# Scripting the start of a DeltaNet and feed-forward kernel: counted conversion steps, denser score evacuations, weight fetches from another queue

## The chip, the core and the metric

The kernel runs on one core of a Trainium2 chip. The time is device microseconds (us) of that core for one execution. Below, VectorE, ScalarE, TensorE and GpSimd are the core's compute engines, and SP is the engine that here only issues transfers (DMAs). Each engine works off its own queue of instructions in order: an instruction that waits holds all that stand behind it in the same queue (in run e8 below one ScalarE step waits 10.78 us for its tile, and the copies behind it come late).

Single executions of one kernel spread over some 1 to 7 us, so medians are quoted with the profile's own span beside them where a trace is argued from.

## The reference, cut to what matters

```python
k_n = k / (norm(k) + 1e-6)                       # q, k, v: (4, 8, 768, 48), float32
for t in range(768):                             # the delta rule, per batch and head
    y[t]  = q[t] @ state
    v_old = state @ k_n[t]
    state = state + beta[t] * outer(k_n[t], v[t] - v_old)
x  = y as (3072, 384)
xn = x / sqrt(mean(x * x) + 1e-6) * rms_g
out = (silu(xn @ w_gate) * (xn @ w_val)) @ w_out # weights are float64: 384x1536, 384x1536, 1536x384
```

The kernel works in chunks of 128 tokens. A unit is one chunk of one batch, so there are 24 units, four to a chunk. For each chunk, K is normalized and transposed, scores are formed on TensorE, the diagonal blocks of the scores are gathered through DRAM into one tile (`gblk`), all 32-by-32 blocks are inverted together on VectorE (31 steps of two operations), and the result is scattered back through DRAM (`td`, `tt`, `nd`, `ne`). Then a short recurrence of matmuls gives each unit's outputs, and the feed-forward follows. The weights arrive as 64-bit words and are turned to float32 by hand: 18 tiles, five VectorE operations and one ScalarE operation each, some 4 us of VectorE a tile.

## The kernel before

The four parts that the change touches. Everything of the first chunk is a generator in one plan with a time for each step; the program's order on each engine comes from these planned times.

```python
def fetch():                                     # one raw weight tile, 768 KB, three buffers
    ...
    nc.sync.dma_start(out=to, in_=src)           # SP's queue, with all other loads

def keys(to, p_g):                               # K's scores, 8 copies a unit, all on ScalarE
    nc.scalar.copy(to[:, :, K0], p_g[:, :, K0])
    nc.scalar.copy(to[hi, :, K1], p_g[hi, :, K1])

def gather(n):                                   # four transfers a unit, issued by ScalarE
    for a in range(NBLK):
        nc.scalar.dma_start(out=gds[c][...], in_=gp[b][W * a : W * (a + 1), :, o : o + W])
    if b == B - 1:
        nc.sync.dma_start(out=gblk, in_=gds.pop(c))
# ... cut ...
TF = 68                                          # planned start of the feed-forward
at(0, setup())
for n in range(B):
    at(0, prepare_first(n, ...))
at(20.9, invert(0, 0.74))
at(49, recur(0, 1.5, 3))                         # units 0,1 and then 2,3
for i, m in enumerate((0, 1, 0, 1)):
    at(TF + CYC // 4 * i, ffn(m, ...))
at(0, weights([(12 + 4.2 * i, 0.8) for i in range(2)] + [(46 + 4.2 * i, 0.8) for i in range(5)]
              + [(TF + 1 + 3.1 * i, 0.6) for i in range(11)]))
```

The preparation of a later unit, which plays a part in the end, is the same in both kernels:

```python
def normalize(n):
    nc.scalar.square(ksq, kn)                    # ScalarE
    nc.vector.tensor_reduce(out=ksum, in_=ksq)   # VectorE
    nc.gpsimd.tensor_scalar_max(ksum, ksum, 1e-30)
    nc.gpsimd.tensor_tensor(out=knrm, in0=ksum, in1=half, op=ALU.pow)   # GpSimd, 1.7 to 2.7 us
    yield
    nc.vector.tensor_scalar_add(knrm, knrm, 1e-6)                       # VectorE waits for it
    nc.vector.reciprocal(krec, knrm)
    ...
def prepare(n):
    norm_k = normalize(n)
    next(norm_k); yield 1.5; next(norm_k); yield 2.5
    transpose(n, qpad[n % 2], Q0);  yield 3
    transpose(n, kpad[n % NK], K0); yield 2
    score(n, ..., both)                          # its masks are VectorE operations
    yield 1
    gather(n)
```

Of the kernel before, what the change touches and what calls it, by code (L numbers as in the profile page):

```python
# [21 lines left out]
W = 32  # L22
# [5 lines left out]
def kernel(  # L28
# [105 lines left out]
    def setup():  # L134
        for t in kpad + qpad:
            nc.vector.memset(t[:, :, D:DP], 0.0)
        for n in range(B):
            load_k(n)
        fetch()

        beta_sb = ttb.rearrange("p k j -> p (k j)")[0:BH, 0:S]
        nc.sync.dma_start(out=beta_sb, in_=beta.rearrange("b h s -> (b h) s"))
        blocks = beta.rearrange("b h (c a i) -> a (b h) c i", a=NBLK, i=W)
        for a in range(NBLK):
            nc.sync.dma_start(out=nbeta[a * BH : (a + 1) * BH], in_=blocks[a])
        load_q(0)
        fetch()
        load_q(1)
        fetch()
        nc.sync.dma_start(out=g_sb, in_=moe_rms_g.rearrange("(t p) -> p t", p=128))  # L150
        nc.vector.memset(half, 0.5)
        nc.vector.memset(mhalf, -0.5)
        make_identity(nc, ident)
        row, col = (
            gblk.bitcast(I32).rearrange("p k j -> p (k j)")[:, C * i : C * (i + 1)] for i in (0, 1)
        )
        nc.gpsimd.iota(row, pattern=[[0, 128]], base=0, channel_multiplier=1)
        nc.gpsimd.iota(col, pattern=[[1, 128]], base=0, channel_multiplier=0)
        nc.vector.memset(mask[lo, 1], 1.0)
        for i, p in enumerate((lo, hi)):  # L160
            nc.vector.tensor_tensor(
                out=mask[p, i], in0=row[p, p], in1=col[p, p], op=ALU.is_lt
            )
        p_fill.append(psum.tile([128, DM], FP32, name="p_fill", tag="out", bufs=2))
        stay_warm(14)
        yield 15
        nc.vector.tensor_scalar(
            out=nbeta, in0=nbeta, scalar1=-1.0, scalar2=None, op0=ALU.mult
        )
        yield 3  # L170
        p_bt = ps_delta([128, NCH, BH], "p_bt")
        for c in range(NCH):
            nc.tensor.transpose(
                p_bt[:, c], beta_sb[:, c * C : (c + 1) * C], ident[0:BH, 0:BH]
            )
        nc.scalar.copy(beta_t, p_bt)
        yield 5
        for n in range(B):
            load_v(n)
        load_k(B)  # L180
        yield 3
        nc.scalar.memzero(tt_all)
        yield 4
        nc.scalar.memzero(gp_all[HC:C, :, 0:HC])
        yield 4
        for t in state:
            nc.scalar.memzero(t)


    p_fill = []  # L190
# [26 lines left out]
    def fetch():  # L217
        i = len(raws)
        if i < len(todo):
            raw = bits.tile([128, WT], I64, name="raw", bufs=3)  # L220
            src = todo[i][1]
            to = raw if len(src.shape) == 2 else raw.rearrange("p (n m) -> p n m", m=DM)
            nc.sync.dma_start(out=to, in_=src)
            raws.append(raw)

    def words(raw):
# [9 lines left out]
        nc.scalar.activation(out=top, in_=high.bitcast(FP32), func=ACTF.Copy, scale=2.0**-112)  # L236
        return top

    def weights(times):
        clock, tops = 0, []  # L240
        for i, ((dst, src), raw, (time, dt)) in enumerate(zip(todo, raws, times)):
            yield time - clock
            clock = time + 5 * dt
            if i == 0:
                tops.append(shrink(raw))
            low, high = words(raw)
            top = tops[i]
            top_u, dst_u = top.bitcast(U32), dst.bitcast(U32)
# [5 lines left out]
                op0=ALU.logical_shift_left,  # L254
                op1=ALU.bitwise_and,
            )
            yield dt
            nc.vector.scalar_tensor_tensor(
                out=top_u,
                in0=high,  # L260
# [2 lines left out]
                op0=ALU.bitwise_and,  # L263
                op1=ALU.bitwise_or,
            )
            yield dt
            if i + 1 < len(todo):
                tops.append(shrink(raws[i + 1]))

            nc.vector.tensor_scalar(  # L270
                out=dst_u, in0=top_u, scalar1=0xFF800000, scalar2=None, op0=ALU.bitwise_and
            )
            yield dt
            nc.vector.scalar_tensor_tensor(
                out=dst, in0=low, scalar=2.0**-52, in1=dst, op0=ALU.mult, op1=ALU.mult
            )
            fetch()
            yield dt
            nc.vector.tensor_tensor(out=dst, in0=dst, in1=top, op=ALU.add)
            yield dt  # L280
        bits_pool.close()


    def normalize(n):
# [66 lines left out]
        keys(to, p_g)  # L351
        queries(to, p_g)

    def bare_queries(to, p_g):
        nc.scalar.copy(to[lo, :, Q0], p_g[lo, :, Q0])
        nc.scalar.copy(to[:, :, Q1], p_g[:, :, Q1])

    def gather(n):
        c, b = divmod(n, B)
        if b == 0:  # L360
            gds[c] = dram.tile([128, W, W], FP32, name="gd")
        for a in range(NBLK):
            o = diagonal(a)
            nc.scalar.dma_start(
                out=gds[c][a * BH + b * H : a * BH + (b + 1) * H].rearrange("h r j -> r h j"),
                in_=gp[b][W * a : W * (a + 1), :, o : o + W],
            )
        if b == B - 1:
            nc.sync.dma_start(out=gblk, in_=gds.pop(c))
# [20 lines left out]
        gather(n)  # L390


    def prepare_first(n, times):
        norm_k = normalize(n)
        yield times[0]
        next(norm_k)
        yield times[1]
        next(norm_k)
        yield times[2]
        transpose(n, kpad[n % NK], K0)  # L400
        yield times[3]
        score(n, crossed((0, slice(K0, K0 + 1)), (1, slice(K0, None, 2))), keys)
        gather(n)
        yield times[4]
        transpose(n, qpad[n % 2], Q0)
        load_q(n + 2)
        yield times[5]
        score(n, crossed((0, slice(Q0, None, 2)), (1, slice(Q1, Q1 + 1))), bare_queries)
        yield times[6]
        for place, p in ((Q0, lo), (Q1, hi)):  # L410
            part = gp[n][p, :, HC * place : HC * (place + 1)]
            nc.vector.tensor_tensor(
                out=part, in0=part, in1=mask[p, place // 2, None].to_broadcast([HC, H, HC]), op=ALU.mult
            )
# [4 lines left out]
    def invert(c, dt):  # L419
# [19 lines left out]
                stay_warm(2, tmp_b[:, 0 : min(128, n * (i + 1))])  # L439
            yield dt  # L440
        if c == 0:
            stay_warm(22)
        td = dram.tile([128, W, W], FP32, name="td")
        nd = dram.tile([128, W, W], FP32, name="nd")
        nc.sync.dma_start(out=td, in_=ttb)
# [32 lines left out]
            if n + B < NU:  # L478
                load_v(n + B)

    def recur(c, dt, warm=0):
        units = range(B)
        vss, x2s, p_zs, us = {}, {}, {}, {}

# [139 lines left out]
        ys = {}  # L624
        if c == 0:

            for a, b in ((0, 1), (2, 3)):
                corner(a, None)
                stay_warm(warm)
                yield dt  # L630
                corner(b, a)
                yield dt
                inner(None, None, a)
                corner(None, b)
                yield dt
                inner(a, None, b)
                stay_warm(warm)
                yield dt
                inner(b, a, None)
                stay_warm(warm)  # L640
                yield dt
                u_a = us[a]
                outer(None, a)
                yield dt
                inner(None, b, None)
                stay_warm(warm)
                yield dt
                u_b = us[b]
                outer(None, b)
                yield dt  # L650
                transpose_y(a, scale(*ys.pop(a)))
                stay_warm(warm)
                yield dt
                transpose_y(b, scale(*ys.pop(b)))
                stay_warm(warm)
                yield dt
                update(a, u_a)
                yield dt
                update(b, u_b)
                reload()  # L660
                dt, warm = 1.2, 0
                yield dt
            return
        for s in range(-3, B + 2):
            inner(s, s - 1, s + 1)
# [98 lines left out]
        yield 0.1  # L764



    plan = []

    def at(time, gen):  # L770
# [2 lines left out]
    def run_plan(until=math.inf):  # L773
        heap = plan
        heapq.heapify(heap)
        while heap and heap[0][0] < until:
            t, i, gen = heapq.heappop(heap)
            dt = next(gen, None)
            if dt is not None:
                heapq.heappush(heap, (t + dt, i, gen))  # L780


    TF = 68
    CYC = 3 * FT * B // 2
    at(0, setup())
    for n in range(B):

        times = (3.5 + 1.2 * n, 6.6 + 1.7 * n, 7.4 + 1.8 * n, 9.3 + 1.8 * n, 24 + 4 * n, 26 + 4 * n, 46.5 + 3 * n)
        at(0, prepare_first(n, [b - a for a, b in zip((0,) + times, times)]))
    at(20.9, invert(0, 0.74))  # L790
    at(49, recur(0, 1.5, 3))
    half_f = FT // 2
    for i, m in enumerate((0, 1, 0, 1)):
        at(TF + CYC // 4 * i, ffn(m, half_f * (i // 2), half_f * (i // 2 + 1)))
    at(
        0,
        weights(
            [(12 + 4.2 * i, 0.8) for i in range(2)]
            + [(46 + 4.2 * i, 0.8) for i in range(5)]
            + [(TF + 1 + 3.1 * i, 0.6) for i in range(11)]  # L800
        ),
    )
    for c in range(1, NCH):
        t0 = TF - 16 + CYC * c
        first = TF + 2 if c == 1 else t0 - 60
        for b in range(B):
            at(first + 4.5 * b, prepare(B * c + b))
        at(first + 27, invert(c, 0.68))
        at(*((t0 - 4, recur(c, 0.9)) if c == 1 else (t0 - 9, recur(c, 1.2))))
        for g in range(B // 2):  # L810
            at(t0 + 16 + CYC // 2 * g, ffn(B // 2 * c + g, 0, FT))
    with tc.manual_schedule():
        run_plan(TF + CYC // 2)
    run_plan()


# [28 lines left out]
```

## Time and profile before

The median is 883.5 us in three runs. The page and the stretches are shown in the prediction, from the same trace (span 881.3 us).

| mark in the trace of before | us |
|---|---|
| first inversion step (VectorE) | 35.33 |
| inversion ended (start of the product after it) | 62.47 |
| first p_w of unit 0 on TensorE | 73.02 |
| first feed-forward matmul | 103.58 |
| TensorE idle from there to 260 | 10.1 |
| clock lost from there to 215 | 4.5 |

Idle is the length of a stretch less TensorE's busy time. Clock lost is the length times one less the mean granted clock; the clock is given to two digits, so it is good to about 0.6 us. Idle time at a low clock counts in both.

### The profile page before, as it was taken

How to read it: one execution, taken by the hardware profiler on the slowest of the kernel's cores; microseconds unless marked ns; L12 is line 12 of the kernel's file. 1: busy time of each engine (PE TensorE's matmuls, PEld its weight loads, DVE VectorE, ACT ScalarE, POOL GpSimd, SP SyncE). 2: the span in 40 equal slices, each digit the busy share in tenths (PEclk: the TensorE clock that was granted, in tenths of full speed). 3: DMA queues.
4: the chain of work that ended last, by engine and by line, in shares of the span. 5: the costliest groups of instructions: out<-in, count | busy, mean ns of one | idle time of the engine just before them, and what ended most of it. 6: DMA issues, size and time to landing. Idle time of an engine off the chain costs nothing.

```text
span 881.3 us, 19880 instructions
## 1 busy us (share of the span) xinstructions
PE 828.5 (94%) x8434; PEld 646.7 (73%) x8434; DVE 404.7 (46%) x997; ACT 259.0 (29%) x691; POOL 97.7 (11%) x136
## 2 busy tenths in 40 slices
PE   6487798989999999999999999999999999999998
PEld 5376665767877777787777787777787777777776
DVE  3786677886243393243392243492332491221110
ACT  4622345511424312324311324212334212221101
POOL 3000144200041000131000131000130000010000
PEclk8576799999999999999999999999999999999999
DMA  7615536502222103122103122103121103000000
GB/s 182 169 45 133 145 98 157 151 2 75 57 56 49 46 18 86 31 63 39 47 18 85 38 56 41 46 18 85 39 55 23 36 23 80 2 20 1 18 1 18
DMA packets 150935, 51.81 MB, mean 59 GB/s; under 512 B 142368, under 2 KB 145440, under 8 KB 150848
## 3 DMA queue, kind: packets, MB, share of 16 engines
q1 hardware_dynamic: 124736, 47.40, 21.2%
q10 hardware_dynamic: 26112, 3.15, 2.2%
q8 instruction: 66, 1.08, 0.5%
q14 instruction: 21, 0.17, 0.1%
HBM read 36.37 MB, written 14.16 MB: 57 GB/s over the span
## 4 chain that ended last, share of the span: by engine, by line
PE 72%; DVE 9%; DMA 2%; ACT 2%; issue 1%; POOL 1%; ACTq 0%; SPq 0%
PE p_gv L732 36%; PE p_o L719 18%; DVE tmp L428 4%; DVE ttb L437 3%; PE p_g L329 3%; PE p_y L531 2%; PE p_t L313 2%; PE p_k L569 2%; PE p_z L587 2%; PE p_y L569 2%; PE p_x L605 1%; PE p_v L497 1%; PE p_z L596 1%; DMA gblk<-gd 1%; PE p_s L550 1%; DVE h_f L743 1%
## 5 line engine op out<-in xcount | busy, mean ns | idle before, releaser
L719 PE MATMUL p_o<-wo_sb,h_f 128*128 128x384 f32 x576 | 215.8, 497 | 11.1 <-DVE h_f L743 11.1
L732 PE MATMUL p_gv<-xt,wg_sb 128*128 128x256 f32 x864 | 217.3, 388 | 0.0
L732 PE MATMUL p_gv<-xt,wv_sb 128*128 128x256 f32 x864 | 213.6, 383 | 0.0
L732 PEld LDWEIGHTS p_gv<-xt,wg_sb 128*128 128x128 f32 x864 | 161.6, 193 | 39.4 <-issue 0.6
L732 PEld LDWEIGHTS p_gv<-xt,wv_sb 128*128 128x128 f32 x864 | 161.5, 190 | 24.4 <-issue 2.5
L743 DVE TENSOR_TENSOR h_f<-sil,p_gv 128x256 f32<-128x256 f32 x144 | 60.1, 418 | 241.3 <-ACT sil L741 241.1
L741 ACT ACTIVATE sil<-p_gv 128x256 f32<-128x256 f32 x144 | 55.1, 383 | 342.8 <-PE p_gv L732 314.7
L719 PEld LDWEIGHTS p_o<-wo_sb,h_f 128*128 128x128 f32 x576 | 104.0, 190 | 62.7 <-DVE h_f L743 16.7
L428 DVE SCALAR_TENSOR_TENSOR tmp<-gblk,nbeta,ttb 128x31 f32<-128x31 f32 (+15 forms) x186 | 74.7, 402 | 11.5 <-DMA gblk<-gd 4.7
L437 DVE TENSOR_TENSOR ttb<-ttb,tmp 128x31 f32<-128x31 f32 (+15 forms) x186 | 63.6, 342 | 6.6 <-PE p_g L329 0.5
L343 DVE TENSOR_TENSOR gp<-p_g,mask 64x128 f32<-64x128 f32 (+1 forms) x160 | 37.9, 277 | 40.0 <-ACT gp L339 35.6
L329 PE MATMUL p_g<-kqt 64*64 64x192 f32 (+2 forms) x896 | 46.3, 331 | 9.5 <-ACT gp L339 4.8
L329 PEld LDWEIGHTS p_g<-kqt 64*64 64x64 f32 x896 | 34.1, 147 | 20.1 <-ACT gp L339 6.5
L293 POOL TENSOR_TENSOR knrm<-ksum,half 128x8 f32<-128x8 f32 x24 | 42.4, 1765 | 2.0
L688 POOL TENSOR_SCALAR ms<-ms 128x1 f32<-128x1 f32 x24 | 5.9, 247 | 328.0 <-ACT y L680 327.8
L318 ACT COPY kqt<-p_t 128x512 f32<-128x512 f32 x48 | 28.0, 584 | 40.2 <-PE p_t L313 37.9
L420 POOL MEMSET ttb<- 128x1024 f32 x6 | 6.1, 1021 | 261.5 <-DMA td<-ttb 246.0
L587 PEld LDWEIGHTS p_z<-v_raw,tt 64*64 64x64 f32 x768 | 26.1, 142 | 8.8 <-issue 6.7
L512 ACT COPY vs<-p_v 32x256 f32<-32x256 f32 x48 | 17.4, 362 | 49.4 <-PE p_w L504 28.1
L338 ACT COPY gp<-p_g 128x128 f32<-128x128 f32 x96 | 25.5, 265 | 20.3 <-PE p_g L329 18.4
L605 PE MATMUL p_x<-tt,gp 64*64 64x64 f32 x384 | 29.0, 229 | 1.8 <-ACT tt L514 1.8
L531 PE MATMUL p_y<-u,gp 128*64 128x48 f32 x768 | 26.6, 222 | 3.4 <-DVE u L612 3.2
(87 smaller groups left out, 798.6 us busy)
## 6 DMA issues: line engine op xcount, KB each, us to landing
kpad<-in_k_dram SPq DMA_DIRECT2D x24, 192.0 KB, 2.6
raw<-in_moe_w_gate_dram SPq DMA_DIRECT2D x6, 768.0 KB, 5.0
qpad<-in_q_dram SPq DMA_DIRECT2D x24, 192.0 KB, 2.8
raw<-in_moe_w_val_dram SPq DMA_DIRECT2D x6, 768.0 KB, 4.7
v_raw<-in_v_dram SPq DMA_DIRECT2D x24, 192.0 KB, 3.0
raw<-in_moe_w_out_dram SPq DMA_DIRECT2D x6, 768.0 KB, 4.3
out_dram<-o_sb SPq DMA_DIRECT2D x24, 192.0 KB, 1.9
gd<-gp ACTq DMA_DIRECT2D x96, 32.0 KB, 1.7
```

Source lines behind the costliest of these rows:

```text
L293: nc.gpsimd.tensor_tensor(out=knrm, in0=ksum, in1=half, op=ALU.pow)
L329: nc.tensor.matmul(to, pair[d, K1 if i else K0], pair[d, places], skip_group_check=True)
L343: nc.vector.tensor_tensor(out=to[p, :, place], in0=p_g[p, :, place], in1=mask[p, i, None].to_broadcast([p.stop, 2, HC]), op=ALU.mult,)
L428: nc.vector.scalar_tensor_tensor(out=tmp, in0=gblk[:, i, None, i + 1 :].to_broadcast(shape), scalar=nbeta[:, c, i : i + 1], in1=ttb[:, 0 : ...
L437: nc.vector.tensor_tensor(out=to, in0=to, in1=tmp, op=ALU.add)
L531: nc.tensor.matmul(p_y[p, h], gp[b_y][:, h, HC * place : HC * (place + 1)], u[:, h], start=(c == 0 and h == 0), stop=True, skip_group_chec ...
L587: nc.tensor.matmul(p_zs[b_z][p, h], tt[b_z][p, h], r[p, h], start=(h == 0), stop=(p is lo), skip_group_check=True,)
L605: nc.tensor.matmul(p_x[lo, h], gp[b_x][hi, h, HC * K0 : HC * (K0 + 1)], tt[b_x][hi, h], skip_group_check=True,)
L719: nc.tensor.matmul(p_o[i], h_f[:, i * C : (i + 1) * C], wo_sb[:, f], start=(f == f0), stop=(f == f1 - 1),)
L732: nc.tensor.matmul(p_gv[:, i], w_sb[:, t, f * 128 : (f + 1) * 128], xt[:, t], start=(t == 0), stop=(t == KT - 1),)
L741: nc.scalar.activation(out=sil, in_=p_gv[:, 0], func=ACTF.Silu)
L743: nc.vector.tensor_tensor(out=h_f, in0=sil, in1=p_gv[:, 1], op=ALU.mult)
```

## The change

Its intent: start the feed-forward sooner. (1) The first chunk becomes a script, and instead of planned times the script says after which instruction how many conversion steps stand on VectorE. (2) K's scores of a unit go to two PSUM banks and leave in four larger copies, two on VectorE and two on ScalarE; SP issues the gathers. (3) All but the first three weight fetches are issued by GpSimd. (4) The second chunk's planned times move. The diff, cut to its core:

```diff
-            nc.sync.dma_start(out=to, in_=src)
+            (nc.sync if i < 3 else nc.gpsimd).dma_start(out=to, in_=src)
...
+        dma = (nc.scalar if c > 0 else nc.sync).dma_start      # in gather
...
+    def keep_keys(n, p_gs):
+        for par in range(2):
+            nc.vector.tensor_copy(out=heads(n, par, K0), in_=p_gs[par][:, :, 0])
+            nc.scalar.copy(heads(n, par, K1)[hi], p_gs[par][hi, :, 1])
+        gather(n)
... the recurrence of units 0 and 1, in one go; 2 and 3 stay in the plan
+            corner(0, None); stay_warm(3); convert(1)
+            corner(None, 0); stay_warm(2); corner(1, None)
+            inner(None, None, 0); convert(1)
... 
+            transpose_y(1, scale(*ys.pop(1)))
+            convert(4)
+            yield
+            update(0, u_0)
...
+        for n in range(B):                                     # in begin
+            p_gs = score_part(n, K0)
...
+            keep_keys(n, p_gs)
+            convert((1, 2, 2, 5)[n])
...  the second chunk; its old places, counted from the feed-forward's start,
...  were 2 + 4.5 * b, 29 with 0.68, 52 with 0.9, and 36 planned units in manual order
+            at((8 if c == 1 else t0 - 76) + 4.5 * b, prepare(B * c + b))
+        at(35 if c == 1 else t0 - 49, invert(c, 0.62))
+        at(*((57, recur(c, 0.7)) if c == 1 else (t0 - 25, recur(c, 1.2))))
+        run_plan(60)
```

## The prediction

> **What bounds the kernel now.** I read the granted clock and busy slices over the span first, then a table by stage, then the engines' timelines up to 104 us.
>
> From the page of the kernel before, each digit one of 40 slices of 22 us:
>
> ```profile
> PE   6487798989999999999999999999999999999998
> ...
> PEclk8576799999999999999999999999999999999999
> ```
>
> TensorE is full from about slice 10 on and neither full nor at full clock before. The table by stage (stretch, its length, then busy us and instruction count of PE, PEld, DVE, ACT and POOL, the granted clock, DMA share, GB/s):
>
> ```profile
> 0.00:36.00 36.00, 21.83 (x218) 17.20 (x218) 16.46 (x42) 20.94 (x56) 10.14 (x18) 0.74 0.65 171
> 36.00:63.00 27.00, 17.05 (x162) 14.22 (x163) 23.09 (x61) 9.84 (x33) 0.00 (x0) 0.65 0.36 75
> 63.00:104.00 41.00, 29.61 (x535) 27.24 (x534) 30.84 (x42) 11.87 (x28) 2.69 (x4) 0.73 0.46 135
> 104.00:200.00 96.00, 86.36 (x671) 65.17 (x671) 74.02 (x158) 38.24 (x92) 23.11 (x21) 0.95 0.40 105
> 200.00:860.00 660.00, 655.73 (x6783) 509.61 (x6782) 258.18 (x692) 175.44 (x478) 61.75 (x93) 1.00 0.18 42
> ```
>
> From 200 us on TensorE idles 4 us in 660: that part can't get shorter, for the change takes no matmul out of it. All to be won lies before the first feed-forward matmul at 103.58 us, and in the 9.6 us of idle (96.00 - 86.36) and the lost clock between 104 and 200. The end is therefore: start of the feed-forward, plus the matmuls left by then, plus TensorE's later idle.
>
> The marks of the path to 103.58, from the timelines of the engines (start, duration in us, engine, what; the wait before it in brackets):
>
> ```profile
> 14.49 1.86 ACTq L364 DMA_DIRECT2D gd<-gp  x4
> ...
> 28.84 1.82 ACTq L364 DMA_DIRECT2D gd<-gp  x4
> ...
> 31.94 0.34 SPq L369 DMA_DIRECT2D gblk<-gd  x1
> ...
> 35.33 0.25 DVE L428 SCALAR_TENSOR_TENSOR tmp<-gblk,nbeta,ttb 128x31 f32<-128x31 f32 x1 [3.61 <-DMA gblk<-gd]
> ...
> 62.47 1.96 DVE L447 TENSOR_TENSOR gblk<-ttb,nbeta 128x1024 f32<-128x1024 f32 x1
> ...
> 84.83 0.56 DVE L612 TENSOR_TENSOR u<-p_z,beta_t 64x384 f32<-64x384 f32 x1 [2.64 <-PE p_z L596]
> ...
> 90.75 0.56 DVE L612 TENSOR_TENSOR u<-p_z,beta_t 64x384 f32<-64x384 f32 x1
> ...
> 103.58 2.68 PE L732 MATMUL p_gv<-xt,wg_sb 128*128 128x256 f32 x6
> ```
>
> K is normalized, transposed and scored (to 28.84), gathered through DRAM (gblk issued at 31.94), inverted on VectorE (35.33 to 62.4, 27.1 us), scattered, and then units 0 and 1 run the recurrence. In the K part ScalarE is the serial engine: from 12.52 to 30.66 it does four times eight small evacuations (0.26 to 0.27 us each, 2.3 us a unit) and four times the issue of four gathers (1.8 us a unit, during which its queue does nothing else). That is 16.4 of the 18.1 us.
>
> **What the Trainium skill says.** "TensorE: Matmul & The Clock Gate", Part 1 (the HAM clock gate): the clock is halved after an idle window of about 3.4 us and restored after a busy one. The trace agrees: the granted clock is 0.65 and 0.73 in the second and third stretch, and four 128x128 transposes take 0.66 us at full and 1.11 at half clock. So the fills stay useful, and idle costs more than its length.
> "DMA: Bandwidth & Descriptors", section "Issuing engines are not separate DMA queues": SP, ScalarE and GpSimd feed the same 16 DMA engines, and another issuer saves sequencer time alone. Hence the gathers moved to SP should land no sooner after issue (median 1.7 us here), but ScalarE gets 1.8 us a unit back; and weight loads issued earlier by GpSimd will share the DMA engines with the gathers.
> "SBUF — State Buffer", section "SBUF: two separate sides": a DMA issued by GpSimd needs descriptors that it can't write while VectorE runs a two-port operation. No fetch is issued by GpSimd in the trace before, so it shows nothing of this. The 128x768 tensor_scalar steps (0.56 us) are candidates for such a lock, and they surround every fetch.
>
> **The change part by part.**
>
> 1. K's scores. A unit's evacuation becomes two VectorE copies of 128x256 and two ScalarE copies of 64x256. From rows reading PSUM (128x256 on VectorE 0.42, 32x256 on ScalarE 0.36) I take 0.40 and 0.37: 0.8 us and 0.75 us side by side, in place of 2.3 us on one engine; the four issues go to SP. ScalarE stops being the bound. But in ScalarE's new order the fourth square stands behind the first transposed copy (end 9.5), so the fourth reduce ends at about 10.6, and in VectorE's order it stands before unit 1's normalization: 11.55 instead of 10.24. From there by hand: transpose of unit 1 to 12.7 (half clock), score 0 to 14.7, its copies to 15.6, one conversion step 0.56, normalization of unit 3 0.93, score 1 to 17.8, copies to 18.6, two steps (0.96 + 0.56) to 20.2, score 2 to 20.9, copies to 21.7, two steps (0.96 + 0.96) to 23.7, copies of unit 3 to 24.5, SP's four issues 1.85 to 26.3, last landing 1.3 later as before (30.66 to 31.94) at 27.6, gblk 3.4 as before: 31.0. Nearby weight loads may add 0.8. The inversion starts at 31.8 and not 35.3: 3.5 us saved. The inversion itself is the same 62 operations: no change.
>
> 2. The recurrence of units 0 and 1. The scatter chain behind the inversion is the same (td, tt, nd, ne by SP), so unit 0's p_w can start hardly before its 10.4 us. From there the script helps: p_w of unit 0 no longer shares its loop with p_v of unit 1, so p_x starts about 1.3 us sooner; and VectorE's order is chosen by hand. Before, u of unit 1 waited from 88.1 (its p_z done) to 90.75 behind a mask and three conversion steps: 2.6 us. In the new order only the mask stands between, and both gains together bring that u from 90.75 to about 86. Following p_y, square, pow, scale, transpose with the old durations (1.2, 0.7, 1.6, 0.6, 0.8) and a fill of 0.9 puts the last x-transposed at about 92 on the old clock of the inversion's end. Then the feed-forward starts at once; before it waited for both state updates and the corners of units 2 and 3, to 103.58. This moves 11.4 us, but the moved matmuls (64 for the states, about 2.4 us, and 96 for the corners, about 2.2) are still to be done, and the sixth weight tile is converted only at about 95.4, a stall of up to 1.2. Left: 11.4 - 4.6 - 1.0 = 5.8 us.
>
> 3. Weight fetches by GpSimd. Before, ScalarE waited 4.5 us for a raw tile at 86.4, because SP's queue was full of scatters; that wait ends. It was beside the path, so it counts only within part 2. Against it, two fetches now fall into the scatter: I take off 0.5 us.
>
> 4. The middle, 104 to 200. Conversions before the feed-forward: six tiles instead of seven and a half, but the rest is done (12 x 3 = 36 units of the plan) about when the second inversion starts (35), while before the two overlapped and h_f stood behind both (3.8 us of idle between 174 and 190, with a half-clock window after it). The second recurrence starts later and runs denser (0.7 for 0.9 a step), which can give a little back. I credit 2 us of the 9.6 plus lost clock.
>
> Sum: 3.5 + 5.8 - 0.5 + 2 = 10.8 us, so 883.5 - 10.8 = 872.7; I say 872.
>
> **The rivals.**
> a) The second recurrence becomes the bound: with fewer feed-forward blocks to hide its chain, TensorE idles around 190 to 230 and the gain of the start is given back. For: in the old trace this stretch has no slack to lose (0.4 us of idle in 200 to 250), and the chain runs through ScalarE and VectorE. Against: the plan ends it at the same time. It would give 878 to 884.
> b) Fetches by GpSimd are late or block GpSimd's queue, where the pow of the norms and the clearing of ttb stand behind them (ttb is cleared after the second fetch, by my count at about 30, one us before it is needed). A slip of 2 us each at the inversion and in the scatter makes 876 to 878.
> c) All of the middle's stalls go: 9.6 us of idle and some 5 of half clock in three windows of 3.4. With parts 1 to 3 that makes about 860. For: the conflict of conversions and inversion is gone. Against: VectorE still has some 72 us of work in order before the inversion, beside some 80 of TensorE's, with GpSimd's pow (1.7 to 2.7 us) in the chain of each norm.
>
> **Range and chances.** Parts 1 and 2 are counted with steps known to about 1.5 and 2 us, part 4 to about 4; together some 5.5. So 864 to 879. Faster by over 2% needs under 865.8, which only c) gives: 0.15. Slower needs a loss of 18 us beyond everything here: 0.02.
>
> **What would show it.** The first inversion step at 31 to 32; its length 27; the last u of unit 1 without a wait behind conversions; the first feed-forward matmul 57 to 61 us after the inversion's start in place of 68; idle between there and 200 us under 9 us; from 200 on the same 4 us in 660. It is wrong if the first inversion step comes after 34 (then fetches or VectorE's steps hold the copies back), if the scatter from the inversion's end to p_w takes over 12 us, or if TensorE idles over 3 us in one piece during the second recurrence.

## The result, and the profile after

The changed kernel takes 878.29 us (median of four, 877.12 to 880.34), beside 883.62 (882.53 to 884.96) for the kernel before: ratio 0.9941, with a 95% interval of 0.9917 to 0.9966. A ratio is the mean time of one kernel's fast runs over that of the other's fast runs of the same rounds, so it is not quite the ratio of the medians quoted. The gain is 5.3 us where 11.5 were forecast. The profiled run spans 878.6 us, 2.7 less than the profiled run of before.

The page of the changed kernel, in the same slices as before:

```profile
PE   7377899798999999999999999999999999999998
...
PEclk8576999999999999999999999999999999999999
```

The clock is up in the fifth slice (88 to 110 us), where it was at 0.7 before. The table of stretches with the same bounds and columns as in the prediction:

```profile
0.00:36.00 36.00, 22.19 (x254) 18.08 (x254) 20.34 (x54) 18.67 (x34) 11.34 (x20) 0.73 0.80 198
36.00:63.00 27.00, 15.72 (x138) 13.76 (x139) 23.27 (x57) 5.71 (x15) 0.00 (x0) 0.66 0.23 54
63.00:104.00 41.00, 32.71 (x487) 28.30 (x485) 27.00 (x39) 12.81 (x27) 4.92 (x9) 0.83 0.50 128
104.00:200.00 96.00, 88.29 (x741) 66.75 (x742) 81.64 (x170) 37.86 (x95) 27.98 (x29) 0.96 0.38 104
200.00:860.00 660.00, 652.42 (x6765) 507.32 (x6764) 256.06 (x685) 174.50 (x476) 61.75 (x93) 1.00 0.18 42
```

From 63 to 104 us TensorE does 3.1 us more and at 0.83 of its clock instead of 0.73: the earlier start. From 104 to 200 it is busy 88.29 us instead of 86.36, though VectorE has 7.6 us more to do there. But from 200 to 860 it idles 7.6 us, and before it idled 4.3: a wait has moved across that mark, as the part on the prediction shows. The marks of the path (start, duration, engine, what; in brackets the wait before it and what ended it):

```profile
28.23 0.34 SPq L364 DMA_DIRECT2D gblk<-gd  x1
...
33.82 0.25 DVE L440 SCALAR_TENSOR_TENSOR tmp<-gblk,nbeta,ttb 128x31 f32<-128x31 f32 x1 [5.96 <-DMA gblk<-gd]
...
61.19 1.93 DVE L459 TENSOR_TENSOR gblk<-ttb,nbeta 128x1024 f32<-128x1024 f32 x1
...
72.38 1.20 PE L516 MATMUL p_w<-vs,ne 32*32 32x32 f32 x32 [4.52 <-DMA ne<-nd]
...
88.78 0.56 DVE L624 TENSOR_TENSOR u<-p_z,beta_t 64x384 f32<-64x384 f32 x1 [0.74 <-PE p_z L608]
...
94.69 1.56 PE L770 MATMUL p_gv<-xt,wg_sb 128*128 128x256 f32 x6 [1.23 <-DVE xt L741]
```

`gblk` is issued 3.7 us sooner than before (31.94), yet the first inversion step comes only 1.5 us sooner, because VectorE waits 5.96 us for it instead of 3.61. From the inversion's end to the first p_w it is 11.2 us, before 10.6. The last u of unit 1 no longer waits behind conversions. The feed-forward starts 8.9 us sooner (94.69 against 103.58), and only 2.7 of them are left in the span.

The table of transfers shows the first loss. Transfers issued from 24 to 36 us (engine of issue, count, size of each, median us from issue to landing), first of the kernel before:

```profile
gblk<-gd SPq DMA_DIRECT2D x1, 512.0 KB, 3.3
gd<-gp ACTq DMA_DIRECT2D x8, 32.0 KB, 1.7
```

Then of the changed one:

```profile
raw<-in_moe_w_val_dram POOLq DMA_DIRECT2D x1, 768.0 KB, 6.1
...
gblk<-gd SPq DMA_DIRECT2D x1, 512.0 KB, 5.5
...
gd<-gp SPq DMA_DIRECT2D x3, 32.0 KB, 3.6
```

The window holds eight of the gathers before and three after; over all sixteen the median is 1.7 us before and 3.1 in the changed kernel. The gathers and the load of `gblk` take about 2 us longer each, while a weight tile is in flight. That suggests theory 1: **GpSimd's fetches, issued as soon as a buffer is free, take DMA time from the gathers and from the scatter.**

For the rest, I worked out what the middle costs. In the changed kernel TensorE idles 13.0 us from the first feed-forward matmul to 260 us, before 10.1. So of the 8.9 us, 3.0 go into idle (13.03 less 10.08) and 3.2 into TensorE's busy time behind the start, mostly matmuls of states and corners that stood ahead of it before. Theories for the idle: theory 2, **VectorE's sheer load** (it is busy 81.6 of 96 us from 104 to 200, and gives an earlier TensorE nothing to work on); theory 3, **the retimed plan** of the second chunk, that is, the order in the queues. Theory 4: fills in the first recurrence that run at half clock before ready work cost 2 us.

### The profile page after: what moved, and what is told of

Same layout as the page of the kernel before. It is cut to its first block, busy times and chain, and to the rows that moved or that the text cites. A ratio compares the mean times of both kernels' runs of the same rounds, so it can differ in the third digit from the quotient of the medians.

```text
span 878.6 us, 19862 instructions
## 1 busy us (share of the span) xinstructions
PE 826.3 (94%) x8438; PEld 645.1 (73%) x8438; DVE 410.0 (47%) x1005; ACT 252.0 (29%) x651; POOL 106.0 (12%) x151
## 4 chain that ended last, share of the span: by engine, by line
PE 77%; DVE 14%; DMA 3%; issue 2%; ACT 2%; POOL 1%; SPq 0%; ACTq 0%; DVEq 0%; POOLq 0%
PE p_gv L770 36%; PE p_o L757 18%; DVE tmp L440 5%; DVE ttb L449 4%; PE p_g L327 3%; PE p_y L543 2%; PE p_z L599 2%; PE p_t L311 2%; PE p_k L581 2%; PE p_x L617 2%; PE p_y L581 2%; PE p_fill L183 1%; PE p_v L509 1%; PE p_z L608 1%; PE p_w L516 1%
## 5 line engine op out<-in xcount | busy, mean ns | idle before, releaser
L327 PE MATMUL p_g<-kqt 64*64 64x192 f32 x640 | 31.7, 331 | 0.3 <-ACT kqt L316 0.3
L599 PE MATMUL p_z<-v_raw,tt 64*64 64x48 f32 x768 | 29.0, 225 | 0.1
L327 PEld LDWEIGHTS p_g<-kqt 64*64 64x64 f32 x640 | 23.2, 132 | 7.4 <-issue 5.5
L617 PEld LDWEIGHTS p_x<-tt,gp 64*64 64x64 f32 x384 | 25.6, 142 | 3.3 <-ACT tt L526 2.3
```

The costliest lines, as they stand in the source:

```text
L327: nc.tensor.matmul(to, pair[d, K1 if i else K0], pair[d, places], skip_group_check=True)
L599: nc.tensor.matmul(p_zs[b_z][p, h], tt[b_z][p, h], r[p, h], start=(h == 0), stop=(p is lo), skip_group_check=True,)
L617: nc.tensor.matmul(p_x[lo, h], gp[b_x][hi, h, HC * K0 : HC * (K0 + 1)], tt[b_x][hi, h], skip_group_check=True,)
```

## The experiments

All twelve in one table first. The start is that of the first feed-forward matmul in the kernel's trace, "idle" and "lost" are defined above, the span belongs to the same trace, the median belongs to its timed runs, the ratio is to the kernel before of the same rounds; each ratio's interval is about 0.0025 to each side.

| kernel | start of feed-forward | idle to 260 | clock lost | span | median | ratio |
|---|---|---|---|---|---|---|
| before | 103.58 | 10.1 | 4.5 | 881.3 | 883.6 | 1 |
| changed | 94.69 | 13.0 | 4.8 | 878.6 | 878.3 | 0.9941 |
| e1 fetches on SP | 90.67 | 12.9 | 6.2 | 875.5 | 874.8 | 0.9904 |
| e2 fetches gated | 88.00 | 13.0 | 3.8 | 870.3 | 872.4 | 0.9877 |
| e3 old plan (wrong result) | 92.35 | 11.9 | 3.7 | 873.2 | 873.9 | 0.9899 |
| e4 one step left out (wrong result) | 95.23 | 9.3 | 1.2 | 871.0 | 870.8 | 0.9860 |
| e5 = e2 without fills | 88.90 | 12.0 | 7.6 | 873.2 | 875.7 | 0.9912 |
| e6 = e2, near the old plan | 88.94 | 11.4 | 1.3 | 869.9 | 870.5 | 0.9862 |
| e7 = e2, gathers by ScalarE | 88.06 | 13.0 | 6.4 | 873.3 | 872.6 | 0.9884 |
| e8 = e2, conversions ahead | 91.74 | 12.2 | 4.9 | 873.7 | 874.6 | 0.9907 |
| e9 = e2, norm apart | 89.50 | 10.8 | 1.3 | 868.2 | 868.8 | 0.9818 |
| e10 = e8 mended | 88.82 | 12.4 | 5.1 | 871.3 | 873.0 | 0.9856 |
| e11 = e10 and e6's plan | 88.34 | 7.8 | 3.8 | 865.3 | 867.1 | 0.9801 |
| e12 = changed, norm apart | 94.02 | 10.8 | 1.2 | 872.9 | 875.4 | 0.9903 |

e2 and e7 have the same middle, and one trace of each lost 3.8 and 6.4 us of clock; a single trace's loss is worth no more than that. The four runs of the changed kernel alone span 875.3 to 878.6 us, and its profiled one is the longest. e1 to e8 ran on one chip (median of before 883.4 to 883.5 us), e9 to e12 on another (884.0 to 885.6): across these two groups the ratios are the fairer measure, with 0.001 worth 0.9 us.

**e1: all fetches back on SP.**

```diff
-            (nc.sync if i < 3 else nc.gpsimd).dma_start(out=to, in_=src)
+            nc.sync.dma_start(out=to, in_=src)
```

> All weight fetches go back to SP's queue (the third part of the change undone, the rest kept). Theory 1 (fetches that GpSimd issues early share the DMA engines with the gathers and with the scatter): the load of gblk lands in about 3.4 us after issue instead of 5.5 and the first inversion step comes at 31 to 32 us instead of 33.8; from the inversion's end to the first p_w 9.7 to 10.4 us instead of 11.2; the first feed-forward matmul about 3 us earlier, 91 to 92, unless fetch 5, now behind the scatter in SP's queue, comes late and stalls the sixth tile by 2 us or more. Rival (the slow gathers have another cause, the dense issue of sixteen gathers by one engine): first step still at 33 to 34. Theory 2 (VectorE's in-order queue sets the pace from 150 to 211 us): the total moves by less than half of what the feed-forward's start moves: 876 to 878.5.

Measured: 874.8 us. The first inversion step comes at 32.67, `gblk` lands 3.3 us after its issue, p_w of unit 0 stands 9.1 us behind the inversion's end, the feed-forward starts at 90.67. The feed-forward moved 4.0 us and the total 3.5: theory 1 holds, and the "less than half" of theory 2 does not. The inversion gained less than hoped, as SP now issues `gblk` only at 29.19: it issued a weight fetch at 22.50, just ahead of the last four gathers, and the two of these that fall after 24 us took 4.8 us to land. So a fetch by SP slows the gathers too.

**e2: GpSimd's fetches, but gated.** GpSimd holds them until a one-column copy of its own has read `gblk`, and later `ne`.

```diff
+        if held: held[0] += 1; return              # in fetch
...
+            if i == 0:                             # before the inversion
+                see(slice(0, 128), gblk[:, 0, 0:1])
+                for j in range(held.pop()): fetch()
...
+        see(slice(64, 96), ne[64:96, H, 0:1])      # behind the inversion
```

> GpSimd still issues the fetches, but fetches 3 and 4 only when gblk has landed and 5 and 6 only when ne of unit 1 has landed. Theory 1: first inversion step at 31 to 32 us, p_w of unit 0 at 9.7 to 10.4 us after the inversion's end, as with all fetches on SP. Theory 2: the total falls by under half of what the start of the feed-forward moves, 875 to 878. If it is only the issuing of DMAs by GpSimd, not their time, that costs, the first step stays at 33 to 34.

Measured: 872.4 us, 5.9 under the changed kernel. Its transfers from 24 to 36 us:

```profile
raw<-in_moe_w_val_dram POOLq DMA_DIRECT2D x2, 768.0 KB, 7.3
...
gblk<-gd SPq DMA_DIRECT2D x1, 512.0 KB, 3.9
...
gd<-gp SPq DMA_DIRECT2D x1, 32.0 KB, 1.6
```

And its marks:

```profile
29.77 0.25 DVE L449 SCALAR_TENSOR_TENSOR tmp<-gblk,nbeta,ttb 128x31 f32<-128x31 f32 x1 [3.61 <-DMA gblk<-gd]
...
57.13 1.96 DVE L468 TENSOR_TENSOR gblk<-ttb,nbeta 128x1024 f32<-128x1024 f32 x1
...
66.20 0.22 PE L525 MATMUL p_w<-vs,ne 32*32 32x32 f32 x2 [2.38 <-DMA ne<-nd]
...
88.00 1.56 PE L779 MATMUL p_gv<-xt,wg_sb 128*128 128x256 f32 x6 [1.23 <-DVE xt L750]
```

The last gather (the only one issued in this window) lands in 1.6 us again and `gblk` in 3.9. Over all sixteen gathers the median is 1.6. The inversion starts 4.05 us sooner than in the changed kernel, sooner also than the 31 to 32 expected, and from its end to p_w it is 9.1 us instead of 11.2. The fetches are still GpSimd's, so it is their time that cost, not their issuer. Theory 1 is shown, with 6.7 us at the start of the feed-forward, and the total keeps nearly all of it (5.9): hardly anything of this earlier start is given back. My expectation of 875 to 878 from theory 2 was wrong.

**e3: the old constants of the second chunk**, with the fetches as in the changed kernel.

```diff
-            at((8 if c == 1 ...   at(35 if c == 1 ..., invert(c, 0.62))   (57, recur(c, 0.7))   run_plan(60)
+            at((2 if c == 1 ...   at(29 if c == 1 ..., invert(c, 0.68))   (52, recur(c, 0.9))   run_plan(CYC // 2)
```

> The plan's constants for the second chunk (start of its preparation, of its inversion and of its recurrence, their steps, and the length of the manually scheduled stretch) go back to what they were before the change, all of the first chunk as changed. Theory 3 (the later, denser second chunk eats the lead): faster than the changed kernel by 2 to 5 us, 873 to 876. Theory 2 (VectorE's queue of conversions, masks and inversion sets the pace whatever the order): within 2 us of the changed kernel, or slower since conversions and inversion interleave again: 877 to 883.

Measured: 873.9 us, but the result was wrong (relative error 0.11). By the plan's own times unit 7's key norm (2 + 13.5 = 15.5) now stands before the update that loads unit 7's K (1 + 13 x 1.2 = 16.6), so the program would read the buffer before it is reloaded; I did not test this by itself, but e6, which keeps that order, is correct. It may be why the change moved these times back. As evidence it is weak; e6 does it validly.

**e4: less work for VectorE.** Its output is wrong, which doesn't matter for the time.

```diff
-            nc.vector.tensor_tensor(out=dst, in0=dst, in1=top, op=ALU.add)
+            if i < 6:
+                nc.vector.tensor_tensor(out=dst, in0=dst, in1=top, op=ALU.add)
```

> A wrong result on purpose: the last of the five conversion steps (the addition, 0.96 us) is left out for the twelve tiles that are converted beside the feed-forward: 11.5 us of VectorE's work less between 92 and 150 us, TensorE's work unchanged. Theory 2: the lead at the end of this stretch is kept, the total falls by 5 to 9 us, to 869 to 873, with the lead over the kernel before at h_f number 26 on of 8 us or more instead of 2.9. Rival (the chain of the second recurrence or its place in the plan sets the end of the stretch): under 2 us, 876 to 878.5.

Measured: 870.8 us, 7.5 under the changed kernel; idle is 3.7 us less and lost clock 3.6, and the lead over before stays at 9.8 us from about the 27th feed-forward block on. That is what theory 2 expected, and I took it for support. But leaving the additions out also changed the order in VectorE's queue, just at the place that e9 is about (see there), so this run can't tell load from order.

**e5: no fills in the recurrence of units 0 and 1**, all seven calls of stay_warm there taken out.

> The kernel with the gated fetches (872.4 us), with all 22 fills of 128 columns left out of the script of units 0 and 1's recurrence. In its trace the fills between p_w of unit 0 and the last transpose took 1.2 + 1.65 + 1.4 + 1.2 + 0.7 + 1.1 = 7.2 us of TensorE, of which some 2 to 2.6 us stood before work that was ready. Theory 4 (fills at half clock lie on the path): the last u of unit 1 comes 2 us sooner, 23 us after the inversion's end instead of 25, the total 870 to 871.5. Rival (without them the clock falls for longer and the small matmuls and transposes run at half clock): the granted clock from 66 to 90 us falls to 0.5 to 0.6, and the first feed-forward matmul comes at the same time or up to 3 us later: 872 to 876.

Measured: 875.7 us, 3.2 more than e2. Stretch 66 to 90 us of e2 (columns as before):

```profile
66.00:90.00 24.00, 20.96 (x341) 18.88 (x342) 13.21 (x21) 7.25 (x16) 3.80 (x8) 0.79 0.47 126
```

And of e5:

```profile
66.00:90.00 24.00, 18.31 (x297) 16.00 (x298) 12.44 (x20) 7.26 (x16) 3.81 (x8) 0.51 0.48 126
```

The first u comes 1.65 us sooner, the last one 0.3, the feed-forward 0.9 later and starts at half clock. The rival is right and theory 4 falls: the fills stand in the way a little and pay for it.

**e6: e2 with a valid plan near the old one.**

```diff
-            at((8 if c == 1 ...   at(35 ..., invert(c, 0.62))     (57, recur(c, 0.7))   run_plan(60)
+            at((5 if c == 1 ...   at(31.5 ..., invert(c, 0.68))   (53, recur(c, 0.9))   run_plan(CYC // 2)
```

> The kernel with the gated fetches, with the second chunk's plan near the old one but valid: its preparation starts at 5 instead of 8, its inversion at 31.5 with steps of 0.68 instead of 35 with 0.62, its recurrence at 53 with 0.9 instead of 57 with 0.7, the manual stretch 36 units long. If the retimed plan is what cost the middle its 3 us (the run with the old constants, which broke the order of a load and gave a wrong result, came out 4 us faster): 867 to 870, with TensorE's idle from the first feed-forward matmul to 260 us under 10.5 us instead of 13. If VectorE's queue is the limit whatever the order: 871 to 875.

Measured: 870.5 us with a correct result, and idle plus lost clock of 12.7 us instead of 16.9. Both limits of the expectation (870, and 10.5 of idle; measured 11.4) were just missed. The median moved 1.9 us, within what the two intervals leave open, so by itself it supports theory 3 only weakly.

**e7: the gathers of the first chunk by ScalarE again**, on e2.

```diff
-        dma = (nc.scalar if c > 0 else nc.sync).dma_start
+        dma = nc.scalar.dma_start
```

> The kernel with the gated fetches, with the first chunk's sixteen gathers issued by ScalarE again instead of SP. Each issue of four held ScalarE 1.8 us before. If the move of the issues was worth something by itself, the copies of units 1 to 3 come later: the load of gblk is issued 2 to 5 us later than 25.7, the first inversion step at 32 to 34 instead of 29.8, the total 874 to 876. Rival (with two copies per unit on each engine ScalarE has the room, since VectorE's conversion steps set the pace of the K part): first step within 1 us of 29.8, the total within 1.5 us of 872.4.

Measured: 872.6 us, the feed-forward at 88.06 as against 88.00. Moving the issues was worth nothing once the copies were split: `gblk` is issued 1.1 us later and the inversion starts 0.7 later (30.44), and the scatter took that up again in these two traces. So by elimination the split of the copies (and VectorE's steps between them) is what part 1 was worth; no run undid the split.

**e8: VectorE's idle stretches filled.** 39 conversion steps instead of 30 ahead of the feed-forward.

```diff
-            convert((1, 2, 2, 5)[n])
+            convert((1, 2, 2, 9)[n])               # while gblk is under way
...
-            inner(None, None, 0); convert(1)
+            inner(None, None, 0); convert(6)       # while unit 0's u is awaited
...
+                tops.append(shrink(raws[3]))       # ScalarE's step for tile 3, before the inversion
```

> A try at a better kernel, on the one with gated fetches: VectorE's idle stretches before the feed-forward are filled with conversion steps: four more while gblk is under way (VectorE waited 3.6 us there), five more while units 0 and 1 wait for their first u (it waited 7.3 us), two behind the last transposed x instead of before it. 39 steps instead of 30 before the feed-forward, so 9 steps, about 7 us, leave the middle. If VectorE's load is what makes TensorE wait between 90 and 215 us, as leaving out 11.5 us of it suggested (7 us gained), the total falls by 3 to 6 us to 866 to 869, and the feed-forward starts 1.5 us sooner without the wait for wv_sb (1.0 us). If the place of the second chunk in the plan is what counts: 871 to 873.

Measured: 874.6 us, slower than e2: a mistake of mine. ScalarE, and then VectorE, in the trace of e8:

```profile
34.29 0.90 ACT L234 ACTIVATE top<-raw 128x768 f32<-128x768 f32 x1 [10.78 <-DMA raw<-in_moe_w_val_dram]
...
50.21 0.47 DVE L449 SCALAR_TENSOR_TENSOR tmp<-gblk,nbeta,ttb 128x240 f32<-128x240 f32 x1 [4.70 <-PE p_fill L183]
```

ScalarE stood 10.78 us for a tile whose fetch was gated. The evacuations of Q's scores behind it came late, TensorE with them, and in the end the inversion waited 4.70 us for a fill that reads its tile. The feed-forward began 3.7 us later. Still, idle in the middle fell by only 0.8 us with nine steps less to do there, which speaks against theory 2.

**e9: e2 with the norm's two halves farther apart.** In the traces of the changed kernel and of e2 the largest single wait in the middle is the same. In the changed kernel:

```profile
158.81 1.67 POOL L291 TENSOR_TENSOR knrm<-ksum,half 128x8 f32<-128x8 f32 x1
...
160.51 1.71 DVE L294 TENSOR_SCALAR knrm<-knrm 128x8 f32<-128x8 f32 x1 [1.88 <-POOL knrm L291]
160.59 2.03 DVE L341 TENSOR_TENSOR gp<-p_g,mask 64x128 f32<-64x128 f32 x4
161.22 0.97 POOL L432 MEMSET ttb<- 128x1024 f32 x1
...
162.55 0.63 PE L311 MATMUL p_t<-ident,kpad 128*128 128x128 f32 x4 [3.01 <-DVE gp L341]
```

VectorE stands 1.88 us for GpSimd's power, and its own operation on it, of 128 by 8, lasts 1.71 us, to 162.22. In VectorE's queue the eight masks of unit 6's scores stand behind that operation (four of them ahead of the reciprocal). The norm is unit 8's, the first of the third chunk: it is the fifth after the start of the feed-forward, and the four before it (squares at 114.82 to 147.76) are those of units 4 to 7. The plan has unit 8's preparation only at 68, behind the part in manual order, and yet its norm stands here. ScalarE had its copies of the same scores by 158.4, so the masks were ready some 2 us before VectorE got to them. TensorE needs the banks that they free for its next key transposes, unit 7's, and waits 3.01 us. In the kernel before, VectorE waits for the same power (1.82 us, to 158.60), but TensorE then has half a feed-forward block and a product (159.07 to 161.76) ahead of these transposes, and does not wait.

```diff
-        next(norm_k); yield 1.5; next(norm_k)
+        next(norm_k); yield 3 if n < 2 * B else 1.5; next(norm_k)
...
-            at((8 if c == 1 else t0 - 76) + 4.5 * b, prepare(B * c + b))
+            at((6.5 if c == 1 else t0 - 76) + 4.5 * b, prepare(B * c + b))
```

> The kernel with the gated fetches (872.4 us), with 3 plan units instead of 1.5 between the first and the second part of the norm of units 4 to 7, and their preparation starting 1.5 units earlier, so that everything behind the norm keeps its place. In the traces of the changed kernel and of the gated one TensorE waits 3.0 us for masked scores before the transposes of unit 7's keys; VectorE's queue stood there 1.89 us for GpSimd's power with the masks behind it. If this order in VectorE's queue is one of the middle's extra costs: that wait falls under 1 us, TensorE's idle from the first feed-forward matmul to 260 us falls from 13.0 to 10 to 11, and the total to 868 to 870.5. If the wait only moves to another place: 871.5 to 874.

Measured: 868.8 us, 3.6 under e2 (5.2 by the ratios). The wait before the transposes is gone, idle is 10.8 and the clock lost 1.3 instead of 3.8. The edit does not touch unit 8's own norm, but moves it in the queue: GpSimd works out two powers back to back (140.43 and 142.52), and VectorE waits for the second one (2.45 us, to 144.22) among the masks of unit 5, where TensorE does not wait for VectorE. Unit 6's masks, at 153.51, have no norm ahead of them. So the question was not put off but asked elsewhere. No VectorE work was taken away, only its order changed: theory 3, in the form of one collision.

**e10: e8 mended.** The ScalarE step for tile 3 stands at inversion step 26.

> The try that filled VectorE's idle stretches with nine more conversion steps, with its mistake mended: ScalarE's first step for the fourth tile stood at the head of the inversion and held ScalarE till 34.3 us for a raw tile that GpSimd fetched only after gblk, the evacuations of Q's scores came late and the inversion stood 4.7 us for a fill. Now that step comes at inversion step 26. Expected: inversion 27.4 us long again, first feed-forward matmul at 86 to 88, and, if VectorE's load is what costs in the middle, a total of 865 to 868; if it is the order in the queues, as the first try suggests (its idle in the middle hardly fell with 7 us less of VectorE's work): 869 to 872, with idle from the first feed-forward matmul to 260 us still 11.5 us or more.

Measured: 873.0 us (868.8 to 873.2). The inversion ends within 0.4 us of e2's again, and the feed-forward starts at 88.82. With nine steps less in the middle idle is 12.4 us, and TensorE's old wait is there unchanged:

```profile
158.47 0.63 PE L320 MATMUL p_t<-ident,kpad 128*128 128x128 f32 x4 [2.98 <-DVE gp L350]
```

With this order in the queue, 7 us of VectorE's work moved out of the middle bought nothing in the medians (0.6 us slower than e2) and 1.9 us by the ratios, inside their intervals. Theory 2 does not explain the loss in the middle.

**e11: e10 and e6's plan together.**

> Both together: the mended ahead-of-time conversion steps and the second chunk's plan near the old one (start 5, inversion 31.5 with 0.68, recurrence 53 with 0.9, manual stretch 36 units). If both gains add, 870.5 less 2 to 5: 865 to 868.5. If the plan's gain came from a chance order of VectorE's queue that the earlier conversions change again: 869 to 873.

Measured: 867.1 us (866.9 to 867.8), ratio 0.9801 with an interval of 0.978 to 0.9821, the fastest correct kernel here, 2% ahead of the kernel before (though the interval does not exclude a little less) and 1.4% by the ratios ahead of the changed one. Idle is 7.8 us. It is 3.4 us under e6 and 6.0 under e10 (5.4 and 4.9 by the ratios), more than either alone gave over e2; with the order right, less VectorE work does help. Which of its waits went for which reason I did not take apart.

**e12: the changed kernel with e9's edit alone**, its fetches as they are.

> The changed kernel itself (878.3 us), fetches as they are, with only the longer place between the two parts of the norm of units 4 to 7 (3 plan units instead of 1.5, begun 1.5 sooner). If the collision at unit 7 costs the same here as with the gated fetches (3.6 us there): the wait of 3.0 us before unit 7's transposes falls under 1 us, idle from the first feed-forward matmul to 260 us falls from 13.0 to 10 to 11.5, and the total to 873 to 876. If fetches and collision hang together: within 1.5 us of 878.3.

Measured: 875.4 us. The same place in its trace:

```profile
147.06 1.67 POOL L291 TENSOR_TENSOR knrm<-ksum,half 128x8 f32<-128x8 f32 x1
...
148.75 0.17 DVE L294 TENSOR_SCALAR knrm<-knrm 128x8 f32<-128x8 f32 x1 [2.45 <-POOL knrm L291]
...
152.29 0.17 DVE L294 TENSOR_SCALAR knrm<-knrm 128x8 f32<-128x8 f32 x1
...
158.05 1.66 DVE L341 TENSOR_TENSOR gp<-p_g,mask 64x128 f32<-64x128 f32 x8
158.67 0.63 PE L311 MATMUL p_t<-ident,kpad 128*128 128x128 f32 x4
```

As in e9, VectorE waits for the last of the powers earlier (to 148.75), unit 6's eight masks take 1.66 us with no norm ahead of them, and TensorE goes on at once. Idle fell from 13.0 to 10.8 and lost clock from 4.8 to 1.2. From 160 to 170 us the granted clock is 1.00 instead of 0.83, which is 1.7 us of that lost clock; another 1.7 stand behind a wait of 2.69 us near 200 us that both traces have and after which the clock fell in one of them only. In all the edit gained the changed kernel 2.9 us in the medians (the ratios 0.9941 and 0.9903 say 3.4, just more than their intervals leave open), apart from the fetches.

## Why the prediction was right or wrong

The range held (878.3 in 864 to 879), and a gain of over 2%, given a chance of 0.15, did not come. The gain was 5.3 us of the 11.5 forecast. Three steps failed: the cost of the fetches beside the gathers and the scatter (0.8 and 0.5 us, measured 4.0 and 2.6), the sooner start of p_x (1.3 us, which did not come), and the gain in the middle (2 us, measured 3.0 of loss in idle). None of the three signs of being wrong showed, if narrowly: the first step came at 33.8 (limit 34), p_w 11.2 us behind the inversion (limit 12), and the one wait over 3 us (3.01) lies ahead of the second recurrence. Of the signs of being right, the first step at 31 to 32, idle under 9 us to 200 (9.1) and 4 us of idle after it (7.6) did not come; the other three did.

- **K's scores (3.5 us forecast, 1.5 measured).** The copies were faster than worked out: in the changed kernel both engines are done with unit 3 by 23.0 us, not 24.5. The failed step is "Nearby weight loads may add 0.8": gathers landing in 3.6 instead of 1.6 us and `gblk` in 5.5 instead of 3.9 put the start at 33.8 where e2 has 29.8, so they added 4.0. Without them the part would have been worth 5.6 us, more than forecast. The part about ScalarE's issues was wrong in its reason: e7 shows that their place is worth nothing once the copies are split.
- **The recurrence.** The forecast put the last transposed x at 92 on the old clock, 29.5 us behind the inversion's end, and 0.5 more for the fetches. (By its own marks that moves 11.6 us, not 11.4.) Measured: the feed-forward starts 33.5 us behind it in the changed kernel and 30.9 in e2. One mis-sized term is the 0.5 us for "two fetches now fall into the scatter": 2.6 us, 2.1 of them before the first p_w. That e2 comes within 1.4 us of the 29.5 is luck, for two other steps were off in opposite directions. From the inversion's end to p_w it took 9.1 us in e2 instead of 10.4, and from p_w to unit 1's u 15.9 us (16.4 in the changed kernel), where the forecast has about 13 (86 less 62.4 and 10.4). The failed step is "p_x starts about 1.3 us sooner". Unit 0's p_x starts 3.3 us behind p_w and not 2.5, because a fill of 1.22 us and unit 1's p_v (1.06) stand ahead of it in TensorE's queue; in e5, without the fills, it is 2.5 again. The other half came as said: u of unit 1 follows that of unit 0 by 3.2 us instead of 5.9.
- **What is still to be done behind the start**: 4.6 us of moved matmuls forecast, 3.2 more busy time measured. A small gain that the forecast had not.
- **Fetches by GpSimd.** Rival (b) had the right place and too small a size: it gave 876 to 878 for a slip of 2 us at each end; the slips were 4.0 and 2.6. Its mechanism was half wrong, since it had the fetches late or blocking GpSimd's queue, while they were early and `ttb` was cleared by 27.95 us, 5.9 before it was needed. The prediction had named their sharing of the DMA engines with the gathers and then given it 0.8 us.
- **The middle (2 us of gain forecast, plus the 1.0 us stall for the sixth tile).** The stall came as said (1.02 us). The gain did not: idle rose from 10.1 to 13.0 us. The failed step is the 2 us drawn from "but the rest is done ... about when the second inversion starts", an argument about amounts of work in plan units. What counted was one collision in VectorE's queue, unit 8's norm ahead of unit 6's masks, worth 3 us with its aftermath at a lower clock. The order was the same before, but there TensorE had other work in hand; no sum of busy times shows this. Rival (a) had the sign and the sum (878 to 884 held), but blamed the chain of the second recurrence; the collision stood before that, in the preparation.
- **From 200 us on** the prediction said 4 us of idle as before; it was 7.6. The extra came before 260 us. Most of it is a wait of 2.69 us at 204.81 for a gated value (`h_f`) that stands behind steps of the second inversion in VectorE's queue; before had its like at 186.41 (2.72 us), so it was moved across the mark rather than made.

The lines for p_x of unit 0, first of the kernel before (p_w at 73.02):

```profile
75.56 1.96 PE L605 MATMUL p_x<-tt,gp 64*64 64x64 f32 x16 [1.32 <-ACT tt L514]
```

Then of the changed one (p_w at 72.38):

```profile
73.51 1.22 PE L183 MATMUL p_fill<-ident 128*128 128x128 f32 x4
...
75.66 1.97 PE L617 MATMUL p_x<-tt,gp 64*64 64x64 f32 x16
```

On the two traces 8.9 us sooner, less 3.2 of work still to do, less 3.0 of idle, is 2.7 us of span, as it must be, since a span is busy time and idle. The runs are the test: e2 gives 5.9 us and e9 another 3.6 (5.7 and 5.2 by the ratios). With both, the kernel stands at 868.8, on the far side of the forecast of 872.

Left open: how much of e4's 7.5 us is order and how much load. In its trace the wait of 3 us before unit 7's transposes is gone too and the lost clock is down to 1.2, as in e12. There unit 6's masks (156.75) stand ahead of unit 8's norm (161.01) in VectorE's queue, so the order did change with the work; no run separates the two. Nor did I look for what puts unit 8's norm where it stands.

## What to carry to other kernels

A bulk load on its own queue is not free because nobody waits for it: it starts as soon as its buffer allows, and here that was just when small latency-bound transfers were under way. Tie its start to the landing of those. And when all engines work in order, look for the single place where a result from a slow engine is asked for ahead of work that is ready and that another engine needs. Moving that question to a place where nobody waits (e9) was worth more than taking 7 us of work away (e10); the work taken away paid only with the order mended too (e11).

## What the Trainium skill lacked or had wrong

- "DMA: Bandwidth & Descriptors", "Issuing engines are not separate DMA queues": right as far as it goes (e7: 88.06 against 88.00 us with another issuer). It names saved sequencer time as the only effect. Lacking: another issuer also lets a bulk load pass the order of the first queue; `gblk` landed in 5.5 us instead of 3.9, and the start of the feed-forward lost 6.7 us (94.69 against 88.00 in e2).
- "SBUF — State Buffer", "SBUF: two separate sides": the starved descriptors of GpSimd's DMAs did not stand out, nor do the runs rule them out. A 768 KB tile fetched by GpSimd landed 6.1 us after issue among the gathers, and by SP in 5.5 in the kernel before; two that GpSimd issued together in e2 took 7.3, beside other loads. The section's rule is that GpSimd or certain operations of VectorE (in a mode with both ports, or with two inputs in SBUF), whichever starts first, keep the shared port pair for the whole instruction while the other blocks. It would fit one place if VectorE's operation is of that kind and a fetch's issue counts as an instruction of GpSimd; whether they do, no run shows. In the changed kernel GpSimd began to issue a fetch at 160.44, VectorE's operation of 128 by 8 (0.17 us elsewhere) began at 160.51, and it lasted 1.71 us, through that issue and the clearing behind it (161.22 to 162.19), to end 0.03 us later. In e2 it again lasted 1.71 us and ended 0.03 us behind the clearing. That the port is the cause was not tested.
- No page read for this case has the cost of asking early in an in-order queue: a 1.88 us wait for GpSimd's power became 3.01 us of TensorE's idle, and moving it away (e12) gained 2.9 us of the kernel.
